# Block 0 of a fused attention and channel-mix kernel: v loaded at once and turned ahead of S, its copies shared by ScalarE and VectorE, and x of block 1 among the first up products

## The chip, the cores and the metric

The kernel runs on one core of a Trainium2 chip. The metric is the device time of one execution in microseconds, smaller is better; the profile's span (first to last instruction) is about 1.8 us less.

## The reference, cut to what matters

```python
# four batches, N = 6208 tokens, C = 256 channels
qn = q / (norm(q, axis=1) + 1e-6);  kn = k / (norm(k, axis=1) + 1e-6)
s = kn^T @ qn / tau                    # 256 x 256 for each batch
a = softmax(s, axis=-1)
x = v @ a                              # 6208 x 256
x_prev = x one token earlier (0 first)
xk = mu_k * x + (1 - mu_k) * x_prev;   xr likewise with mu_r
k = relu(xk @ w_k);  out = sigmoid(xr @ w_r) * (k * k @ w_v)
```

S needs all tokens of a batch, so the kernel first streams q and k of batch 0, and nothing of the channel mix can run before S, its softmax and the first x. After that blocks of 512 tokens pass through x, up (w_k), square and down (w_v), while S of the next batch is summed up beside them.

## The kernel before

These are the parts that the change touches. `take_half` copies half of the turned v out of PSUM, `product` makes x and its difference to the token before from the attention shares and v, `mix_first` makes xk and xr, `up_first` makes half a column block of the first up products, `x_half` makes half of x of a later block.

```python
def v_load(i):
    ...
    if i == 0:
        for a in range(2):
            nc.gpsimd.dma_start(v_bf[:, 2 * a:2 * a + 2], v[b, a * H:(a + 1) * H, :].rearrange(
                "(s p) c -> p s c", p=P))
        ...
def v_first():
    vT_ps = ps.tile([P, S, 2, P], BF16, name="vT_ps", tag="kT_ps", bufs=3)   # one PSUM bank
    def turn_half(a):
        for s in (2 * a, 2 * a + 1):
            for h in range(2):
                nc.tensor.transpose(vT_ps[:, s, h], v_bf[:, s, h * P:(h + 1) * P], ident)
    def take_half(a, copy):
        copy(vT0[:, :, a * H + 1:(a + 1) * H + 1].rearrange("c h (s p) -> c s h p", s=2),
             vT_ps[:, 2 * a:2 * a + 2])
...
# order of the loads on the GpSimd queue: v(0), v(1), w_k, q and k, w_r, v(2), w_v, v(3), ...
root(1); root(0)
nc.scalar.activation(gate, ones[:, 0:1], AF.Exp)     # loads the table for exp
turn_half, take_half = v_first()
invert_first(0)
evac_first()                  # VectorE scales S
turn_half(0)
turn()                        # TensorE turns S
turn_half(1)
keep_warm(2)
go = v_transpose_pe(1, nc.scalar.copy)
invert_first(1)
take_half(0, nc.vector.tensor_copy)
difference(0)
exp()
go()
weigh_first(0); weigh_first(1)
take_half(1, nc.vector.tensor_copy)
difference(1)
for a in range(2):
    for ih in range(2):
        product(a, ih)
    for dh in range(2):
        mix_first("xk", a, dh)
...
# main loop, round i == -1:
if i == -1 and j < 3:
    for fh, a in (((0, 0), (1, 0), (0, 1)), ((1, 1),), ())[j]:
        up_first(fh, a)
    if j == 2:
        up(0, 2)
...
if j in (0, 2) and full:
    x_half(n, int(j > 0))     # n = i + 2, here block 1
```

## Time and profile before

| what | value | from |
|---|---|---|
| time | 505.04 us, median of 4 runs, 504.71 to 505.17 | runs |
| span of the profiled run | 503.1 us | profile |
| TensorE busy | 482.3 us, 96% | page, part 1 |
| TensorE idle from 36 to 45 us | 1.93 us | busy time by stage |
| x of block 2 starts | 49.12 us | timeline |

The page's part 1 has each engine's busy time, part 4 the shares of the chain that ended last. Their lines, the table by stage and the chain are in the prediction below. The reading in short: the view of waits lists none of TensorE's matmuls from 49.3 to 480 us, so the change can gain only by starting that stream earlier, and at most the idle time ahead of it.

### The profile page before, as it was taken

The numbers are of one execution on the slowest core, as the hardware profiler recorded it, in microseconds if no ns is written. First come the engines' busy times: TensorE is split into PE (matmuls) and PEld (weight loads), VectorE is DVE, ScalarE is ACT, GpSimd is POOL, SyncE is SP. The second block draws the span as 40 slices with busy tenths as digits, with TensorE's granted clock in tenths as the row PEclk, the third lists the DMA queues.
The fourth block names the chain that finished last, engine by engine and source line by source line (L and its number), as shares of the span: only waits on it lengthen the run. The fifth ranks groups of instructions, "written<-read, shape, count | busy, mean of one in ns | idle before, by whom it ended". The sixth has DMA issues, their size and how long they took to land.

```text
span 503.1 us, 9303 instructions
## 1 busy us (share of the span) xinstructions
PE 482.3 (96%) x3437; PEld 331.2 (66%) x3437; DVE 429.7 (85%) x787; ACT 428.2 (85%) x871; POOL 96.9 (19%) x143
## 2 busy tenths in 40 slices
PE   2789999999999999999999999999999999999996
PEld 1355677677666766666776666676666666666675
DVE  2788899999988998999889899899888787878784
ACT  4788999899999989888999898988888888788884
POOL 0044322222233132122123323100031010000000
PEclk9999999999999999999999999999999999999999
DMA  8999999999799999997799999982295658344123
GB/s 328 418 314 197 196 185 176 209 210 195 149 187 179 202 166 177 146 203 116 142 191 146 197 171 183 168 150 65 66 207 103 152 86 156 77 105 86 56 71 106
DMA packets 131558, 83.46 MB, mean 166 GB/s; under 512 B 50548, under 2 KB 125624, under 8 KB 130488
## 3 DMA queue, kind: packets, MB, share of 16 engines
q0 software_dynamic: 55840, 33.01, 49.8%
q1 hardware_dynamic: 75352, 49.59, 39.9%
q8 instruction: 27, 0.44, 0.4%
q10 hardware_dynamic: 320, 0.26, 0.2%
q14 instruction: 19, 0.16, 0.1%
HBM read 78.71 MB, written 25.43 MB: 207 GB/s over the span
## 4 chain that ended last, share of the span: by engine, by line
PE 92%; DMA 4%; ACT 2%; DVE 1%; issue 0%; SPq 0%; ACTq 0%; DVEq 0%
PE vr_ps L603 33%; PE kT_ps L571 33%; PE vr_ps L599 8%; PE xT_ps L465 8%; PE s_ps L293 6%; DMA f<-in_k_dram 4%; ACT k L160 1%; PE s_ps L199 1%; ACT qk L155 1%; PE st_ps L353 0%; PE y_ps L643 0%; PE kT_ps L511 0%; PE bank L217 0%; PE vT_ps L425 0%; DVE xk L498 0%
## 5 line engine op out<-in xcount | busy, mean ns | idle before, releaser
L576 ACT ACTIVATE kr<-kT_ps 128x512 bf16<-128x512 f32 (+1 forms) x390 | 234.9, 604 | 33.4 <-PE kT_ps L571 29.7
L603 PE MATMUL vr_ps<-w_v_sb,kk 128*128 128x256 bf16 x1536 | 230.3, 273 | 0.0
L571 PE MATMUL kT_ps<-xk,w_k_sb 128*128 128x512 bf16 (+1 forms) x780 | 229.8, 377 | 0.0
L603 PEld LDWEIGHTS <-kk 128*128 128x128 bf16 x1536 | 150.3, 98 | 57.3
L584 DVE TENSOR_TENSOR kk<-kr 128x2048 bf16<-128x2048 bf16 (+1 forms) x148 | 125.7, 850 | 0.2 <-ACT kr L576 0.2
L613 DVE SCALAR_TENSOR_TENSOR res<-res,vr_ps 128x256 f32<-128x256 f32 x192 | 80.0, 416 | 50.1 <-ACT res L612 50.1
L571 PEld LDWEIGHTS <-w_k_sb 128*128 128x128 bf16 x780 | 75.5, 98 | 27.5 <-issue 0.6
L612 ACT ACTIVATE res<-vr_ps 128x256 f32<-128x256 f32 x192 | 76.7, 399 | 1.3 <-PE vr_ps L603 1.3
L599 PE MATMUL vr_ps<-w_r_sb,xr 128*128 128x256 bf16 x384 | 73.3, 273 | 0.0
L467 ACT CAST xT<-xT_ps 128x512 bf16<-128x512 f32 x94 | 55.9, 595 | 20.0 <-PE xT_ps L465 19.7
L556 DVE SCALAR_TENSOR_TENSOR xr<-delta,mu_t,xT 128x512 bf16<-128x512 bf16 x94 | 70.0, 746 | 0.0
L556 DVE SCALAR_TENSOR_TENSOR xk<-delta,mu_t,xT 128x512 bf16<-128x512 bf16 x94 | 70.0, 745 | 0.0
L599 PEld LDWEIGHTS <-xr 128*128 128x128 bf16 x384 | 37.6, 98 | 44.5 <-issue 0.2
L133 POOL DMA_DIRECT2D qk<-in_q_dram x39 | 26.0, 668 | 169.3 <-ACT kr L576 147.7
L465 PE MATMUL xT_ps<-vT,a_sb 128*128 128x512 bf16 x188 | 55.9, 379 | 0.0
L293 PE MATMUL s_ps<-qk 128*128 128x256 bf16 (+1 forms) x294 | 55.8, 273 | 0.0
L254 ACT ACTIVATE sq<-qk 128x1024 bf16<-128x1024 bf16 x48 | 51.0, 1063 | 0.0
L408 POOL DMA_DIRECT2D v_bf<-in_v_dram x47 | 35.6, 759 | 67.3 <-DMA vT<-v_bf 48.7
L199 PE MATMUL s_ps<-qk 128*128 128x384 bf16 (+2 forms) x98 | 20.2, 357 | 14.8 <-ACT qk L155 14.8
L546 DVE TENSOR_TENSOR delta<-xT 128x1024 bf16<-128x1024 bf16 x47 | 32.2, 686 | 1.1 <-ACT xT L467 1.1
L293 PEld LDWEIGHTS <-qk 128*128 128x128 bf16 (+1 forms) x294 | 28.5, 98 | 5.6 <-issue 0.8
L133 POOL DMA_DIRECT2D qk<-in_k_dram x39 | 25.9, 665 | 3.4 <-DMA w_k_sb<-in_moe_w_k_dram 2.0
(113 smaller groups left out, 252.7 us busy)
## 6 DMA issues: line engine op xcount, KB each, us to landing
out_dram<-res SPq DMA_DIRECT2D x47, 512.0 KB, 4.7
v_bf<-in_v_dram POOLq DMA_DIRECT2D x47, 256.0 KB, 7.3
qk<-in_q_dram POOLq DMA_DIRECT2D x36, 256.0 KB, 6.1
qk<-in_k_dram POOLq DMA_DIRECT2D x36, 256.0 KB, 7.3
f<-in_q_dram SPq DMA_DIRECT2D x4, 1024.0 KB, 13.3
f<-in_k_dram SPq DMA_DIRECT2D x4, 1024.0 KB, 11.0
f<-in_q_dram SPq DMA_DIRECT2D x3, 512.0 KB, 7.6
f<-in_k_dram SPq DMA_DIRECT2D x3, 512.0 KB, 6.2
```

What stands on the lines that cost most here:

```text
L133: nc.gpsimd.dma_start(rows_at(qk, b, g, i)[:rows, :n], qk_src(t, b, g))
L293: nc.tensor.matmul(s_ps[:, ih, :], rows_at(qk, b, g, 0)[:rows, s, ih * P:(ih + 1) * P], rows_at(qk, b, g, 1)[:rows, s, :], start=t0 and ih ...
L465: nc.tensor.matmul(xT_ps, a_sb[:, b, ih, dh * P:(dh + 1) * P], vT[:, :, ih, :], start=ih == 0, stop=ih == 1)
L467: nc.scalar.copy(xT[:, dh, 1:], xT_ps)
L556: nc.vector.scalar_tensor_tensor(o[:, dh], st[i, "d"][:, dh], mu[:, dh:dh + 1], st[i, "x"][:, dh, :M], op0=OP.mult, op1=OP.add)
L571: nc.tensor.matmul(kT_ps[:, :m], w_k_sb[:, dh, fh * P:(fh + 1) * P], xk[:, dh, :m], start=dh == 0, stop=dh == 1)
L576: nc.scalar.activation(kr, kT_ps[:, :m], AF.Relu, scale=0.5 ** 0.5)
L584: nc.vector.tensor_tensor(st[i, "kk"][:, fh // 4 * 4 + lo:fh + 1, :m], kr, kr, op=OP.mult)
L599: nc.tensor.matmul(vr_ps[:, D:], xr[:, dh, s * P:(s + 1) * P], w_r_sb[:, dh, :], start=dh == 0, stop=dh == 1)
L603: nc.tensor.matmul(vr_ps[:, :D], kk[:, fh, s * P:(s + 1) * P], w_v_sb[:, fh, :], start=fh == 0, stop=fh == 7)
L612: nc.scalar.activation(res[:, s], vr_ps[:, D:], AF.Tanh, scale=0.5)
L613: nc.vector.scalar_tensor_tensor(res[:, s], res[:, s], 1.0, vr_ps[:, :D], op0=OP.add, op1=OP.mult)
```

## The change

Its intent is to take the turning and the second copy of v off the path from S to the first products, and to fill TensorE's hole among the first up products with x of block 1. The diff is complete but for its context lines:

```diff
 def v_load(i):
-        if i == 0:
-            for a in range(2):
-                nc.gpsimd.dma_start(v_bf[:, 2 * a:2 * a + 2], v[b, a * H:(a + 1) * H, :].rearrange(
-                    "(s p) c -> p s c", p=P))
-            st[i, "v"] = v_bf
-            return
         nc.gpsimd.dma_start(v_bf, v[b, t * M:(t + 1) * M, :].rearrange(...))
...
     turn_half(0)
+    turn_half(1)
+    take_half(0, nc.scalar.copy)
     turn()
-    turn_half(1)
     keep_warm(2)
...
-    take_half(0, nc.vector.tensor_copy)
+    take_half(1, nc.vector.tensor_copy)
     difference(0)
...
-    take_half(1, nc.vector.tensor_copy)
     difference(1)
...
-                for fh, a in (((0, 0), (1, 0), (0, 1)), ((1, 1),), ())[j]:
+                for fh, a in (((0, 0), (1, 0)), ((1, 1),), ())[j]:
                     up_first(fh, a)
+                if j == 0:
+                    x_half(1, 0)
+                    up_first(0, 1)
...
-                if j in (0, 2) and full:
+                if j in (0, 2) and full and (i, j) != (-1, 0):
                     x_half(n, int(j > 0))
```

Below, parts (a) to (d) are those of the prediction: (a) one load, (b) both halves turned ahead of S, (c) ScalarE takes the first half, (d) x of block 1 among the up products.

## The prediction

> **What bounds the kernel now.** I read the page first, parts 1 and 4, for the engine that sets the end.
>
> ```profile
> PE 482.3 (96%) x3437; PEld 331.2 (66%) x3437; DVE 429.7 (85%) x787; ACT 428.2 (85%) x871; POOL 96.9 (19%) x143
> PE 92%; DMA 4%; ACT 2%; DVE 1%; issue 0%; SPq 0%; ACTq 0%; DVEq 0%
> ```
>
> TensorE is 92% of the chain that ended last. The view of waits, asked for TensorE alone from 49.3 to 480 us, lists no wait of a matmul at all, so from there on the kernel is one unbroken stream of matmuls. A change ahead of that stream can only move its start; whatever the start moves should reach the end unchanged. So I then asked for the busy time by stage around the change (columns: stretch, its length, busy us and instruction count of each engine, clock, DMA share, GB/s).
>
> ```profile
> 36.00:39.00 3.00, 2.22 (x23) 1.41 (x21) 2.44 (x8) 2.25 (x6) 3.00 (x5) 1.00 1.03 166
> 39.00:42.00 3.00, 2.26 (x22) 1.69 (x20) 2.37 (x9) 1.95 (x5) 0.82 (x2) 1.00 1.11 191
> 42.00:45.00 3.00, 2.59 (x16) 1.25 (x14) 2.92 (x8) 2.60 (x9) 1.56 (x3) 1.00 1.20 205
> 45.00:48.00 3.00, 3.00 (x24) 1.88 (x23) 1.94 (x3) 2.90 (x7) 1.02 (x2) 1.00 1.44 195
> ```
>
> Between 36 and 45 us TensorE is not full: 3.00 less 2.22, 2.26 and 2.59 leave 0.78 + 0.74 + 0.41 = 1.93 us idle. That is a ceiling on the gain (0.4% of the time). The clock is full throughout. Last I read the chain in order of time there (start, us, engine, tile, line).
>
> ```profile
> 37.38 0.83 PE st_ps L353 x4
> 38.20 0.24 PE vT_ps L444 x4
> 38.44 0.03 issue
> 38.47 0.44 DVE vT L447
> 38.90 0.02 issue
> 38.93 0.43 DVE delta L479
> ...
> 39.92 0.35 DVE a_sb L374
> 40.28 0.34 DVE vT L447
> 40.62 0.04 issue
> 40.66 0.50 PE x_ps L487 x3
> ...
> 42.84 0.39 ACT kr L513
> 43.23 0.04 issue
> 43.27 0.40 PE kT_ps L511 x2
> ```
>
> The turning of v (L444, after S is turned at L353) and both copies of it by VectorE (L447, at 38.47 and 40.19) are on the chain, and so is the wait of the first up product's second half (L511, 43.27) for ScalarE's relu at 42.84. These are the three things that the change touches.
>
> **What the Trainium skill says.** (1) "PSUM — Partial Sum Buffer", section PSUM bank collisions raise a hardware error, has the rule to guard PSUM with semaphores by bank, not by address. The trace agrees that such waits exist: the first half of v was turned by about 36.6, but its copy started at 38.47, just after the second half was turned at 38.44, in the same bank; and L511 at 43.27 waits for the relu of the other half of its own bank. (2) "ScalarE: Activation LUTs", section What ACT_TABLE_LOAD costs, gives 186 + 0.833 N ns for an instruction with immediate scale and bias: 613 ns for the new 128x512 copy (estimate). The trace agrees: 1.01 us for 128x1024 (the rule gives 1.04) and 0.59 for a 128x512 cast. (3) "DMA: Bandwidth & Descriptors", section Issuing engines are not separate DMA queues: all transfers share the 16 DMA engines. Here the DMA share is above 1.0 in every stage shown, so one issue instead of two saves issue time but hardly transfer time.
>
> **The change, part by part.** I write new times in the frame of the old trace and subtract at the end.
>
> (a) v of block 0 in one load. The old issues took 0.86 and 0.73 us from 31.88 and landed after 4.3 and 3.8 us, that is at 36.2 and 36.5. A whole load of the same pattern issues in about 0.75 (as the later ones do). The packets are the same and in the same order, so I take the landing as 36.0 to 36.5. Every later load is issued up to 0.8 us earlier; none of them is waited for now, so this gains nothing by itself.
>
> (b) Both halves turned ahead of S. Four turns issue in some 0.24 us (the chain's row of L444), eight in 0.45. From 36.5 that ends at about 36.95, with results near 37.15. S can be turned only at 37.38, when VectorE has scaled it. So this fits in idle TensorE time, with 0.4 us to spare, and takes 0.24 us out from behind L353.
>
> (c) The first half taken by ScalarE. It is free from the gate's exponential to exp:
>
> ```profile
> 37.33 0.21 ACT L741 ACTIVATE gate<-ones 128x1 bf16<-128x1 bf16 x1
> 38.27 0.47 ACT L361 ACTIVATE e_sb<-st_ps,rn 128x256 f32<-128x256 f32 x1 [0.73 <-PE st_ps L353]
> 43.71 0.38 ACT L513 ACTIVATE kr<-kT_ps 128x256 bf16<-128x256 f32 x1 [0.21 <-PE kT_ps L511]
> 44.14 0.59 ACT L467 CAST xT<-xT_ps 128x512 bf16<-128x512 f32 x1
> 48.07 1.01 ACT L433 COPY vT<-vT_ps 128x1024 bf16<-128x1024 bf16 x1
> ```
>
> From 37.54 a copy of 0.60 ends at 38.14; exp needs S turned, at 38.24. So it is hidden, by 0.1 us. VectorE copies the second half when its reciprocal ends (38.18) and ScalarE is out of the bank (38.14): start 38.20, not 38.47, a gain of 0.27. The difference starts at 38.66, the first reciprocal at 39.00, the first share at 39.19 (its exp and sum are ready at 38.83), the second share at 39.65, ending at 40.00. VectorE no longer has to copy v at 40.19. The products of the second shares (L487, 40.66) waited for that copy; now they wait for the share alone, 40.00 + 0.05 = 40.05. **Gain 0.61 us** (0.27 from the earlier start, 0.34 from the copy gone). The second difference ends near 40.36, before 40.49 when it is needed. The casts of x (L491), the four mixes of xk and the first up products follow at once, so all shift by 0.61; ScalarE's copy of v of block 1, which ends at 40.35, is out of the way of the first cast at 40.58.
>
> (d) x of block 1 between the up products. In the old frame the first four up products end their issue at 42.86. The next needs the relu at 43.23 and the fourth mix, at about 43.35: a hole of 0.4 us. The two products of x take 0.43 (L465 at 43.51 to 43.94) and fit in it. So the third pair goes at 43.29 to 43.51, the fourth to 43.75, the next up product to 44.18. The second x product waited at 44.78 for the cast that ended at 44.73 (same buffer). ScalarE now does that cast right after two relus, 43.55 to 44.14, so TensorE can go at 44.18: 0.60 earlier. But **ScalarE takes over as the limit**. From 42.84 it has the same sum of work in another order, and only its own hole of 0.21 us (before 43.71), with perhaps 0.1 of a later one, can close. It is then gapless to its copy of v of block 2, which moves from 48.07 to 47.76 and ends at 48.77. In the old trace x of block 2 started at 49.12, just after that copy ended at 49.08: no slack. Now it starts at 48.81 and TensorE waits there for about 0.29. So of 0.60 only **0.31 us** remain.
>
> The sum is 0.61 + 0.31 = 0.92 us. From 49 us on both engines shift alike and no transfer comes too late: the closest are w_k (34.00 + 7.0 = 41.0, needed at 41.5 after the shift), v of block 2 (36.48 + 9.1 = 45.6, needed at 46.3) and w_v (37.0 + 11.2 = 48.2, needed at 49.3). So 505.05 - 0.92 = 504.13; I say 504.2, as more small waits can appear than vanish.
>
> **The rivals.**
> 1. v lands late. S is now turned behind all of v, so TensorE would hold S until v is there. For: v used to land only 0.9 us ahead of S, while the DMA engines are over-subscribed, and the first half could start alone. Against: the same packets are queued 0.8 us earlier as to the second half. A landing at 37.5 instead of 36.5 would delay S by some 0.6 and eat part (c): about 504.7.
> 2. ScalarE does not bind. If the buffers of up products leave more slack than I see, part (d) keeps its 0.60: about 503.85. For: in the old trace TensorE never waits after 45 us. Against: the 0.04 us between the end of the copy and x of block 2.
> 3. ScalarE's copy delays exp. It has 0.1 us of slack; if the copy takes 0.8 rather than 0.6, exp and all behind it slip by 0.1 and the second copy, kept out of the bank, too: about 504.35.
> 4. The gain is given back later, to the transfers: the DMA share is 1.44 at 45 to 48 us and some rows of q and k land 2 to 3 us ahead of use. A stream that starts 0.9 earlier has that much less slack. Against: no wait of TensorE from 49.3 to 480. It would leave 504.6 to 505.
>
> **Range and chances.** Rivals 1, 3 and 4 bound the small gains, rival 2 the large. The three old runs lie within 0.14 us, so noise is not the issue. I take 503.7 to 504.8 as the range. A change of 2% is 10 us, while all idle time of TensorE in these stages is 1.93 us: faster by 2% is out of the question, and slower by 2% would take a wait on each of many blocks, which the change does not touch. Faster 0.01, within 2% 0.98, slower 0.01.
>
> **What would show it.** In the new profile: v landing before 36.9 and L444 as one run of eight ahead of L353 at about 37.38; one ScalarE copy of 0.6 us between the gate and exp, with exp still near 38.27; one VectorE copy at 38.2; the second group of L487 near 40.05; x of block 1 (L465) directly behind four L511 and no wait for ScalarE at the fifth; ScalarE gapless from 42.2 to 60; the ScalarE copy of v of block 2 near 47.15 (48.07 - 0.92); and a matmul stream without waits after 49. Wrong would be: S turned later than 37.5, exp later than 38.4, a wait for DMA on TensorE, or a start of x of block 2 later than 48.4, with the time above 504.8.

## The result, and the profile after

The changed kernel took 503.74 us (median of 4 runs, 503.54 to 503.94) against 505.04. The ratio is 0.9975, 95% interval 0.9958 to 0.9993. Ratios here are the mean time of one kernel's runs over that of the other's of the same rounds, so not quite the ratio of the medians quoted. The gain of 1.30 us by the medians is larger than the 0.84 predicted, and the time lies inside the range, near its lower end.

Single executions of both kernels scatter more than the first runs showed. In all four sets the kernel before had medians of 504.85 to 505.07, but single runs up to 508.53; the changed kernel's three sets had medians of 503.74, 503.97 and 504.26, that is 1.30, 1.05 and 0.59 us under the kernel before of the same set. So the gain is about 1 us, and the prediction's 0.84 is not separable from it. The first and third sets of experiments ran on one chip, the second (load_only, rows4, both_dve, act_extra) on another and without the changed kernel beside it, so its kernels are compared through the kernel before.

All lines of the new kernel from the load of v on are numbered six lower (L444 is now L438, L511 is L505, and so on). First the page of the changed kernel, parts 1 and 4:

```profile
PE 478.7 (95%) x3378; PEld 331.0 (66%) x3437; DVE 428.6 (85%) x786; ACT 429.0 (85%) x872; POOL 96.7 (19%) x142
PE 91%; DMA 4%; ACT 2%; DVE 1%; issue 1%; SPq 0%; ACTq 0%; DVEq 0%
```

Some matmul records are missing from this trace (3378 of 3437, while all weight loads are there), so TensorE's lower busy time says nothing. Then its busy time by stage, columns as before:

```profile
36.00:39.00 3.00, 2.37 (x25) 1.58 (x24) 2.44 (x11) 2.97 (x9) 2.57 (x5) 1.00 1.00 156
39.00:42.00 3.00, 2.28 (x18) 1.52 (x18) 2.26 (x9) 2.17 (x7) 0.55 (x2) 1.00 1.09 202
42.00:45.00 3.00, 2.94 (x17) 1.65 (x17) 2.44 (x7) 2.88 (x10) 1.50 (x3) 1.00 1.20 203
45.00:48.00 3.00, 2.95 (x24) 2.01 (x24) 2.80 (x4) 3.00 (x7) 1.58 (x3) 1.00 1.43 196
```

TensorE's hole from 42 to 45 us is nearly closed (2.94 where it was 2.59): that is part (d). Ahead of 42 us it has nearly the holes of before, in other places. The chain in order of time shows them (start, us, engine, tile, line):

```profile
37.57 0.21 ACT gate L735
37.77 0.51 ACT vT L441
38.28 0.02 issue
38.31 0.44 DVE vT L441
38.74 0.02 issue
38.77 0.43 DVE delta L473
...
39.72 0.97 PE x_ps L481 x7
...
41.12 0.89 DVE xk L492 x2
42.01 0.04 issue
42.05 0.49 PE kT_ps L505 x3
42.54 0.43 PE xT_ps L459 x2
```

The second copy at 40.28 and the turning behind S are gone, but ScalarE's copy now stands on the chain ahead of VectorE's. The timeline of the changed kernel shows why, and what S waited for:

```profile
36.77 0.88 DVE L332 TENSOR_SCALAR s_sb<-s_ps,rn 128x256 f32<-128x256 f32 x2
37.03 0.62 PE L438 MATMUL vT_ps<-ident,v_bf 128*128 128x128 bf16 x8 [0.58 <-DMA v_bf<-in_v_dram]
37.49 0.65 PE L353 MATMUL st_ps<-ident_f,s_sb 128*128 128x128 f32 x4
38.31 0.43 DVE L441 COPY vT<-vT_ps 128x512 bf16<-128x512 bf16 x1 [0.35 <-ACT vT L441]
```

v came at 37.0, not by 36.5. TensorE turned v first, as the program orders it, and S at 37.49, that is 0.72 after VectorE began to scale S; in the kernel before it was 37.38 - 36.84 = 0.54. So S was 0.18 late. And VectorE waited 0.35 us for ScalarE to leave the bank.

The gain can be read in three intervals, which the starts in the timelines give: the **front**, from the scaling of S (L332) to the first mix of xk; the **middle**, from there to x of block 2; and the **tail**, from there to the end of the span. "S late" is the start of S's turning (L353) less that of its scaling, less the 0.54 of the kernel before.

| kernel | S late | front | middle | tail | span |
|---|---|---|---|---|---|
| before | 0 | 41.60 - 36.84 = 4.76 | 49.12 - 41.60 = 7.52 | 453.98 | 503.1 |
| changed | 0.18 | 41.12 - 36.77 = 4.35 | 48.06 - 41.12 = 6.94 | 454.14 | 502.2 |

Front 0.41, middle 0.58, tail -0.16, and S's scaling 0.07 earlier: together 0.90, the difference of the spans. The same table for the experiments follows them.

### The profile page after: what moved, and what is told of

Same layout as the page of the kernel before. It is cut to its first block, busy times and chain, and to the rows that moved or that the text cites. A ratio compares the mean times of both kernels' runs of the same rounds, so it can differ in the third digit from the quotient of the medians.

```text
span 502.2 us, 9243 instructions
## 1 busy us (share of the span) xinstructions
PE 478.7 (95%) x3378; PEld 331.0 (66%) x3437; DVE 428.6 (85%) x786; ACT 429.0 (85%) x872; POOL 96.7 (19%) x142
## 4 chain that ended last, share of the span: by engine, by line
PE 91%; DMA 4%; ACT 2%; issue 1%; DVE 1%; SPq 0%; ACTq 0%; DVEq 0%
PE vr_ps L597 33%; PE kT_ps L565 31%; PE vr_ps L593 10%; PE xT_ps L459 8%; PE s_ps L293 6%; DMA f<-in_k_dram 4%; ACT k L160 1%; PE s_ps L199 1%; ACT qk L155 1%; PE y_ps L637 0%; PE st_ps L353 0%; ACT L735 0%; PE vT_ps L419 0%; PE x_ps L481 0%; PE kT_ps L505 0%
## 5 line engine op out<-in xcount | busy, mean ns | idle before, releaser
L565 PE MATMUL kT_ps<-xk,w_k_sb 128*128 128x512 bf16 (+1 forms) x722 | 217.3, 377 | 0.0
L593 PEld LDWEIGHTS <-xr 128*128 128x128 bf16 x384 | 37.6, 98 | 44.6 <-issue 0.2
L402 POOL DMA_DIRECT2D v_bf<-in_v_dram x48 | 36.8, 767 | 97.9 <-DMA vT<-v_bf 49.3
```

The lines of the kernel that those rows point to most:

```text
L565: nc.tensor.matmul(kT_ps[:, :m], w_k_sb[:, dh, fh * P:(fh + 1) * P], xk[:, dh, :m], start=dh == 0, stop=dh == 1)
L593: nc.tensor.matmul(vr_ps[:, D:], xr[:, dh, s * P:(s + 1) * P], w_r_sb[:, dh, :], start=dh == 0, stop=dh == 1)
```

## The experiments

Twelve experiments ran, in three sets. The kernel before ran beside each, with medians of 505.02 (first set), 505.07 (second) and 504.85 us (third). All gave right results.

### after_again and after_third: the changed kernel again

No edit.

> The changed kernel once more, as the yardstick for the three runs beside it on the same chip. Expected: 1.2 to 1.4 us under the kernel before, as in the result on record (503.74 against 505.04). Its profile should tell whether the late start of the softmax of batch 0 in the first profile of the changed kernel (the norms end at 35.97 us, 35.74 in the kernel before; the last loads of q and k landed 0.5 us later) belongs to the change or to that one execution: if to the change, it is again near 36.0; if to the execution, near 35.7.

> The changed kernel a third time, beside the two candidates, and one more sample of the landing of one whole load. So far six executions with one load of 512 rows of v had it at 36.3, 37.0, 37.0, 37.4, 37.7 and 37.7 us, and the three with two loads had all that they waited for by 36.5. Theory L (one load is systematically later): v at 37.0 or later again. Rival (the execution's luck, through the backlog of the q and k loads): by 36.5 as likely as not. Time: 503.7 to 504.0 us.

after_again: 503.97 us, ratio 0.9981 (0.9967 to 0.9995). after_third: 504.26 us, ratio 0.9990 (0.9977 to 1.0002), so by itself its set does not settle a difference. The late start of the softmax in the first execution (scaling of S at 36.77) does not belong to the change: it began at 36.60 and 36.59 in these. v came at 37.0 in the one and at 36.6 in the other, and S was late by 0.37 and by 0. The fronts are 4.59 and 4.36 and the middles 6.93 and 6.94. after_third started its stream earliest of the three, x of block 2 at 47.89, and yet its span is 502.3: its tail is 0.43 longer than before, of which 0.24 is one wait that the timeline shows (start, length, engine, line, tile, and the idle time before with its releaser):

```profile
78.39 0.59 PE L459 MATMUL xT_ps<-vT,a_sb 128*128 128x512 bf16 x2 [0.24 <-DMA vT<-v_bf]
```

The transposing load for this block was issued at 61.02 and landed 17.3 us later; in the kernel before its like was issued at 62.14 and landed after 12.9. In the other twelve traces it landed after 12.7 to 17.2 us. So a transfer that had 4 us of slack (62.14 + 12.9 = 75.0, needed at 79.10) is now sometimes the next limit.

### d_only: part (d) alone

The kernel before with the last three pieces of the diff.

```diff
-                for fh, a in (((0, 0), (1, 0), (0, 1)), ((1, 1),), ())[j]:
+                for fh, a in (((0, 0), (1, 0)), ((1, 1),), ())[j]:
                     up_first(fh, a)
+                if j == 0:
+                    x_half(1, 0)
+                    up_first(0, 1)
...
-                if j in (0, 2) and full:
+                if j in (0, 2) and full and (i, j) != (-1, 0):
```

> The kernel before with only the reordering of x of block 1 among the first up products. Theory A (ScalarE had slack, and the part is worth what the wait view and the hole say): 0.55 to 0.6 us faster than the kernel before, the second product of x of block 1 and x of block 2 both 0.6 earlier. Theory B (as predicted: ScalarE takes over): x of block 1 is 0.6 earlier, x of block 2 only 0.3, and the time falls by 0.3.

504.67 us, ratio 0.9988 (0.9976 to 1.0). The front is the old one (4.76), and the middle fell by only 0.14 to 7.38. That looks like theory B, but the timeline names another cause:

```profile
42.58 0.61 PE L511 MATMUL kT_ps<-xk,w_k_sb 128*128 128x256 bf16 x4 [0.65 <-DMA w_k_sb<-in_moe_w_k_dram]
```

w_k landed at 42.54 in this execution, not at 41.0 as in the profile of before, and the first up products waited for it. From these four to x of block 2 it is 48.77 - 42.58 = 6.19 us, without a wait, so ScalarE did not bind here. Neither number of the two theories came true.

### no_d: parts (a) to (c) without (d)

The changed kernel with the three pieces of d_only taken back.

> The changed kernel without the reordering: only the load at once, both halves turned ahead of S, and the copies shared. Theory A: 0.6 to 0.75 us faster than the kernel before, and 0.55 to 0.6 slower than the changed one. Theory B: 0.6 faster than before, and 0.3 slower than the changed one (which would leave 0.4 of the measured 1.3 unexplained).

505.13 us, ratio 0.9998 (0.9983 to 1.0013): no gain at all. In its trace v landed at 37.7, later than in any profile before:

```profile
37.73 0.62 PE L438 MATMUL vT_ps<-ident,v_bf 128*128 128x128 bf16 x8 [1.22 <-DMA v_bf<-in_v_dram]
```

S was turned at 38.19, 0.83 late, and the front became 5.01, longer by 0.25 than before. The middle is 7.52, exactly that of before. So without (d) the middle is 7.52 and with it 6.94, whatever the front does: **part (d) is worth 0.58 us**. (The medians of no_d and after_again, of the same set, are 1.16 us apart. Their traces differ by 1.1, of which 0.42 is the front, longer in no_d as v came later.) Of the two theories A is right about this term and wrong about the front.

### halves: the changed kernel with v in two loads

```diff
+        if i == 0:
+            for a in range(2):
+                nc.gpsimd.dma_start(v_bf[:, 2 * a:2 * a + 2], ...)
+            st[i, "v"] = v_bf
+            return
```

> The changed kernel, but v of block 0 in two loads as before. Theory L (one load lands later than two: 37.0 us in the changed kernel's profile against 36.2 and 36.5, and S was turned 0.19 us after its scaling was done): v lands by 36.6, S is turned as soon as it is scaled, and the time is 0.15 to 0.25 us under the changed kernel. Rival (the late landing was that execution's, as its loads of q and k were late too): v lands within 0.2 us of the landing in the repeat of the changed kernel, and the times agree within 0.1 us.

504.63 us, ratio 0.9987 (0.9975 to 0.9999). The theory of the landing seemed right: the halves were there at 36.1 and 36.5, S was late by 0, and the front is 4.33. But the time was no better than the changed kernel's (504.63 against 503.97 in the same set). In the trace w_k took v's place:

```profile
41.83 0.61 PE L511 MATMUL kT_ps<-xk,w_k_sb 128*128 128x256 bf16 x4 [0.52 <-DMA w_k_sb<-in_moe_w_k_dram]
```

Two issues for v put that of w_k at 34.05, against 33.7 in the changed kernel, and it landed at 41.8. The middle is 7.24. Later it also waited for the transposing load, issued at 61.09 and landing 17.2 us later.

### load_only: part (a) alone

The kernel before without the branch for block 0 in the load of v.

> The kernel before with v of block 0 in one load and nothing else. Theory L (one load lands later than two; three whole loads so far landed at 37.0, 37.0 and 37.7 us, three pairs of halves by 36.5): v lands at 37 to 37.7, the first four turns wait for it, S is turned up to 0.5 us after it is scaled, and the time is 0 to 0.4 us above the kernel before. Rival (the load's form doesn't matter): v by 36.5, S turned at once, same time.

504.85 us, ratio 0.9988 (0.9964 to 1.0012): not told apart from the kernel before. In the trace v was at 37.7, S 0.59 late, and the front 5.13, longer by 0.37, with the span at 503.4. So the trace shows the loss that was expected, and the times don't resolve it.

### rows4: v with four neighbouring rows in a partition

```diff
-            "(p s) c -> p s c" if i in (1, 2) else "(s p) c -> p s c", p=P))
+            "(p s) c -> p s c" if i in (0, 1, 2) else "(s p) c -> p s c", p=P))
...
-            copy(vT0[:, :, a * H + 1:(a + 1) * H + 1].rearrange("c h (s p) -> c s h p", s=2),
-                 vT_ps[:, 2 * a:2 * a + 2])
+            copy(vT0[:, :, a * H + 1:(a + 1) * H + 1].rearrange("c h (p s) -> c h p s", s=S),
+                 vT_ps[:, :, :, a * P // 2:(a + 1) * P // 2].rearrange("c s h p -> c h p s"))
```

> The changed kernel, but v of block 0 loaded with four neighbouring rows of 256 in each partition, as v of blocks 1 and 2 is, and put in order by the two copies (strided on VectorE and ScalarE). Theory P (the queue of the casting loads moves so many packets in a time, not so many bytes): a quarter of the packets for v, so v lands by 36.5, S is turned as soon as it is scaled, w_k lands 0.3 to 0.5 us earlier than the 41.7 of the changed kernel, the VectorE copy takes up to 0.2 longer, and the time is 0.2 to 0.6 under the changed kernel. Rival (bytes or order set the landing): v at 37.0 again, w_k at 41.7, and the time is the changed kernel's or 0.1 to 0.2 above it for the strided copies.

504.40 us, ratio 0.9982 (0.9958 to 1.0006), with the best trace of all (span 502.0) and two of six executions over 505.5. v was at 36.2, w_k at 41.0 and S not late. From 34.3 to 37.0 us the casting queue moved 0.44 MB in 246 packets, against 0.47 MB in 591 packets in the changed kernel. So it does not move a fixed number of packets in a time, and theory P fails in its reason. The landings that it foretold came true all the same, but v took 4.4 us from issue to landing just as in act_extra, which has the form of the changed kernel, and w_k was issued earlier (32.99 against 33.74) and landed after 8.0 us against 7.9. And VectorE pays for the strided copy:

```profile
36.21 0.62 PE L438 MATMUL vT_ps<-ident,v_bf 128*128 128x128 bf16 x8
...
37.95 0.69 DVE L441 COPY vT<-vT_ps 128x512 bf16<-128x512 bf16 x1
```

The copy takes 0.69 where it took 0.43, and the front is 4.59, 0.25 longer than act_extra's with v as early. The times don't show it to beat the changed kernel.

### both_dve: both halves copied by VectorE

```diff
     turn_half(1)
-    take_half(0, nc.scalar.copy)
     turn()
...
+    take_half(0, nc.vector.tensor_copy)
     take_half(1, nc.vector.tensor_copy)
     difference(0)
```

> The changed kernel with both halves copied by VectorE, one after the other, behind its reciprocal and ahead of the differences; ScalarE copies none. In the changed kernel VectorE waited 0.35 to 0.54 us for ScalarE's copy (same bank), so two copies of 0.43 from 37.96 would end at 38.85, against 38.74. Theory A (the gain of part b and c is from taking the copy of the second half off the time after the shares; who copies matters little): 0.1 us slower than the changed kernel. Rival (as predicted, ScalarE's help brings 0.27 of it): 0.3 to 0.45 slower.

504.03 us, ratio 0.9971 (0.9949 to 0.9993). By the medians it is 1.04 us under the kernel before, within the changed kernel's 0.59 to 1.30; the ratio is lower since two runs of the kernel before in this set took 506.60 and 508.53. v was at 37.4, S 0.56 late:

```profile
38.09 0.89 DVE L441 COPY vT<-vT_ps 128x512 bf16<-128x512 bf16 x2
```

From the turning of v (37.44) to the end of the copies it is 38.98 - 37.44 = 1.54 us; in the changed kernel 38.74 - 37.03 = 1.71. So when v is late, VectorE alone is 0.17 faster, since a copy by ScalarE of 0.59 stands ahead of its own rather than beside it. The front is 4.58, and at a lateness of 0.56 that is 0.2 better than after_again's 4.59 at 0.37 would let expect. That fits theory A; with v early both_dve has no trace, so whether ScalarE's help pays then is not shown.

### act_extra: half a microsecond more for ScalarE

```diff
                 up(i + 1, j)
+                if (i, j) == (-1, 3):
+                    nc.scalar.copy(spare, fill)
```

(The line that makes the tile `spare` is cut.)

> The changed kernel with one more copy of 128x512 on ScalarE (some 0.5 us, into a spare tile) behind the fourth relu of block 0. Theory A (ScalarE has slack there, since in the kernel before it waited for TensorE inside a merged row of relus): x of block 2 is at most 0.1 later and the time the same. Theory B (the reordering has used ScalarE's slack up; its copy of v of block 2 ends at 48.02 us and x of block 2 starts at 48.06): x of block 2 is 0.4 to 0.5 later and so is the end. Either way it says how much of the reordering's 0.58 us a busier ScalarE would have taken.

504.20 us, ratio 0.9976 (0.9954 to 0.9998). Here v was at 36.3 and the front 4.34, but the middle is 7.43, longer by 0.49 than with (d) alone. From the second product of x of block 1 to x of block 2, first in this kernel and then in the changed one:

```profile
43.46 0.59 PE L460 MATMUL xT_ps<-vT,a_sb 128*128 128x512 bf16 x2
48.30 0.59 PE L460 MATMUL xT_ps<-vT,a_sb 128*128 128x512 bf16 x2
```

```profile
43.72 0.59 PE L459 MATMUL xT_ps<-vT,a_sb 128*128 128x512 bf16 x2
...
48.06 0.59 PE L459 MATMUL xT_ps<-vT,a_sb 128*128 128x512 bf16 x2
```

That is 4.84 against 4.34: the copy's 0.5 us (ScalarE's next instruction starts 0.51 after it) comes out in full. Theory B is right that ScalarE has no slack left after the change, though reaching this point cost nothing.

### halves_w_k and whole_w_k: w_k in two loads

```diff
-    nc.gpsimd.dma_start(w_k_sb, moe_w_k.rearrange("(ko ki) f -> ki ko f", ki=P))
+    for f in (slice(0, DF // 2), slice(DF // 2, DF)):
+        nc.gpsimd.dma_start(w_k_sb[:, :, f], moe_w_k.rearrange("(ko ki) f -> ki ko f", ki=P)[:, :, f])
     next_load()
-    nc.gpsimd.dma_start(w_r_sb, moe_w_r.rearrange("(ko ki) d -> ki ko d", ki=P))
     v_load(2)
+    nc.gpsimd.dma_start(w_r_sb, moe_w_r.rearrange("(ko ki) d -> ki ko d", ki=P))
```

The first is halves with this edit, the second the changed kernel with it.

> The changed kernel with v of block 0 in two loads, w_k in two loads of 512 columns each (the first up products need only the first), and w_r behind v of block 2. Theory W (with v in two loads the wait for v is replaced by one for w_k, which is issued 0.5 us later: the first up product waited for w_k at 41.83 and 42.58 us in the two kernels with two loads and the reordering): now v lands by 36.5, w_k's first half by 40.8, no up product waits for a load, the first starts 4.8 us after the scaling of S does, and the time is 0.3 to 0.6 under the changed kernel. Rival (some other load takes the place, most likely v of block 1 at 38.7 or of block 2 at 46.3, as the queue moves the same bytes): the time is that of the changed kernel within 0.2 us, with a wait of TensorE for one of these.

> The changed kernel with w_k in two loads of 512 columns and w_r behind v of block 2, v of block 0 in one load. Theory W: with the whole load it is v that binds and w_k lands just in time (41.7), so the split gains at most 0.1 us; 503.6 to 504.0. Rival (w_k costs the changed kernel more than its profile shows, in other executions than the profiled one): 0.2 to 0.4 us under the changed kernel.

halves_w_k: 504.39 us, ratio 0.9988 (0.9974 to 1.0001). whole_w_k: 504.12 us, ratio 0.9984 (0.9972 to 0.9997). Neither is shown to beat the changed kernel of the same set (504.26, 0.9990). In halves_w_k the second half of v came at 37.3, though it was a load by itself, so two loads do not make all of v early; whether one load is later on the average stays open. The first half of w_k landed at 41.8 in spite of the split, and v of block 2 became a wait:

```profile
46.84 0.62 PE L425 MATMUL vT_ps<-ident,v_bf 128*128 128x128 bf16 x8 [0.28 <-DMA v_bf<-in_v_dram]
```

In whole_w_k v was at 37.6, S 0.77 late, and the front 4.95. The rival of the first expectation, that another load takes the place, came true.

### before_again: the kernel before, one look

No edit.

> The kernel before once more, one look, for a further sample of the landing with two loads (36.2 and 36.5 us in the profile of before) and of w_k (41.0). Theory L: both halves by 36.6. Rival (luck): one of them at 37 or later. In either case the first four turns start near 36.2 and S is turned 0.54 us after its scaling starts, as only the first half is ahead of it.

505.12 us, one run. The first half of v was at 36.4, and S was not late. TensorE turned the second half at 37.95 without a wait, so it was there by then, but no record says when. w_k landed at 42.56, and the first up products waited 0.55 us for it; the kernel before lost 0.27 of that (middle 7.79), as its mixes of xk were only just done.

### All traces side by side

v is the time at which its first turns start, in kernels with two loads that of the first half.

| kernel | v | S late | front | middle | tail |
|---|---|---|---|---|---|
| before | 36.20 | 0 | 4.76 | 7.52 | 453.98 |
| before_again | 36.41 | 0 | 4.76 | 7.79 (w_k late) | 454.00 |
| d_only | 36.15 | 0 | 4.76 | 7.38 (w_k late) | 454.03 |
| load_only | 37.68 | 0.59 | 5.13 | 7.53 | 453.96 |
| no_d | 37.73 | 0.83 | 5.01 | 7.52 | 453.95 |
| changed | 37.03 | 0.18 | 4.35 | 6.94 | 454.14 |
| after_again | 37.05 | 0.37 | 4.59 | 6.93 | 454.08 |
| after_third | 36.61 | 0 | 4.36 | 6.94 | 454.41 |
| halves | 36.08 | 0 | 4.33 | 7.24 (w_k late) | 454.28 |
| rows4 | 36.21 | 0 | 4.59 | 6.94 | 454.03 |
| both_dve | 37.44 | 0.56 | 4.58 | 6.94 | 454.09 |
| act_extra | 36.29 | 0.01 | 4.34 | 7.43 | 454.00 |
| whole_w_k | 37.63 | 0.77 | 4.95 | 6.94 | 454.04 |
| halves_w_k | 36.10 | 0.46 | 4.65 | 7.39 (v of block 2 late) | 454.40 |

## Why the prediction was right or wrong

The time, the direction and the size were right. Of its working some steps held and some did not: parts (b) and (c) were priced about 0.2 us too high with v in time, and more with v late, and part (d) 0.27 too low. That the sum came out near is to that extent luck.

**What bounds the kernel, and that a start moves the end: right.** The tail is 454.0 us, within 0.2, in eleven of the fourteen traces. In after_third, halves and halves_w_k it is 0.3 to 0.4 longer, with a wait for a late transfer named by the timeline or the chain in each (a transposing load in the first two, w_v in the third).

**(a), v by 36.0 to 36.5: wrong, and the most important error.** The step "the packets are the same and in the same order, so I take the landing as 36.0 to 36.5" failed. In eight executions with one load of this form v came at 36.3, 36.6, 37.0, 37.0, 37.4, 37.6, 37.7 and 37.7 us. It is a spread of 1.4 us, where the plan had 0.4 to spare. Where v came at 37 or later, S was turned late, by 0.18 to 0.83 us: rival 1, which was priced at 0.6 for a landing at 37.5, is what happened in most of them. What sets the landing is open. It is not simply one load instead of two: a second half came at 37.3 in halves_w_k. The traces hold one hint. In the three of the eight executions in which the scaling of S began at 36.53 to 36.60, v was issued at 31.87 to 31.95 and came at 36.3, 36.6 and 37.0; in the five in which it began at 36.77 to 36.82, v was issued at 32.11 to 32.16 and came at 37.0 to 37.7. The scaling needs the last of q and k, so v seems to be late when they are; no experiment tested it. The kernel before is less exposed, since only its first half stands ahead of S, and that came at 36.1 to 36.4 in every execution with two loads.

**(b) and (c), 0.61 us: too large.** With v in time the front fell from 4.76 to 4.33 to 4.36, that is by 0.40 to 0.43 us, in halves, act_extra and after_third. The term of 0.34 for the vanished second copy nearly held; the term of 0.27 for an earlier first copy did not. From the scaling of S to VectorE's first copy it was 38.47 - 36.84 = 1.63 us before and 38.05 - 36.53 = 1.52 in act_extra, so 0.11 of the 0.27 came, and from that copy to the first mix of xk it was 3.13 and 2.82, a gain of 0.31.

The failed step is "ScalarE is out of the bank (38.14)", that is ahead of VectorE. VectorE waited for ScalarE by 0.35 us in the changed kernel, 0.54 in after_again, and still 0.36 in act_extra, where v was in time. The Trainium skill's "PSUM — Partial Sum Buffer" (section PSUM bank collisions raise a hardware error) has it that two engines must be kept apart in a bank, on the same partitions, even when both only read. Both copies read all 128 partitions of one bank, and the traces agree that they are kept apart: VectorE's starts 0.03 us after ScalarE's ends, at 38.31 and 38.28 in the changed kernel. I counted that wait, but with ScalarE's copy ending 0.04 us ahead of VectorE's turn; in act_extra it ended 0.33 behind it.

Both times were read from one atypical profile. In act_extra ScalarE's copy started 37.45 - 36.53 = 0.92 us after the scaling of S began; I had 37.54 - 36.84 = 0.70, as a tiny add of VectorE ahead of that scaling (L325) took 0.47 us in that profile, where it took 0.17 in all thirteen other traces. And its second add took 0.34, where it took 0.16 in act_extra, so that VectorE was free 1.16 us after the scaling began and not 1.34. The copy itself was as estimated (0.57 to 0.59, estimate 0.60). In the traces of the changed kernel and no_d with v late, the front gained 0.17 to 0.41 or lost up to 0.25.

**Rival 3, exp delayed by ScalarE's copy: no.** With S turned late, exp started 0.68 us after S's turning did in the changed kernel (38.17 - 37.49), and 0.65 after it in load_only and both_dve, where ScalarE copies no half of v. With S in time it was 0.86 in act_extra and 0.87 in before_again.

**(d), 0.60 in the first place: right.** The hole was filled as told, and the middle fell by 0.58 us in every trace with the reordering that lost nothing to a late load or to the extra copy. **The 0.29 taken off for ScalarE: wrong**, so rival 2 was right. The failed step is "only its own hole of 0.21 us (before 43.71), with perhaps 0.1 of a later one, can close". I read four relus of ScalarE as one gapless piece since the timeline had merged them in one row. Asked for shorter stretches, the view of the kernel before shows that the last of the four starts later than its turn:

```profile
46.86 1.31 ACT L576 ACTIVATE kr<-kT_ps 128x512 bf16<-128x512 f32 x2
```

```profile
47.57 0.60 ACT L576 ACTIVATE kr<-kT_ps 128x512 bf16<-128x512 f32 x1
```

Two starts 0.71 apart, where the others follow in about 0.5: ScalarE waited some 0.2 us for its up product, which TensorE had finished at 47.53. Also its hole before 43.71 is 0.31 by the starts (the two relus at 42.84 took 0.66 together and 0.38 each, so they follow in 0.28, and the third's turn was at 42.84 + 0.56 = 43.40), not the 0.21 that the wait view lists. ScalarE had thus half a microsecond to give, and its copy of v of block 2 moved from 48.07 to 47.01, as much as TensorE's work. That it is now full is shown by act_extra.

**No other transfer too late: wrong for w_k.** It was taken from one landing at 41.0. In the traces it came at 41.0 to 42.6, and in d_only, halves and before_again it cost 0.27 to 0.44 us of the middle. v of block 2 cost about 0.45 in halves_w_k. That a transposing load would be the one to give some of the gain back (rival 4 in kind) was not seen: 0.24 us in after_third.

So in the three traces of the changed kernel the sum 0.61 + 0.31 = 0.92 came about as roughly 0.2 to 0.4 in front, 0.58 in the middle, and 0.1 to 0.4 given back in the tail, while the scaling of S, from which the front is counted, began anywhere from 36.44 to 36.84 in the fourteen traces. Part (d) is the firm share of the gain; parts (a) to (c) pay only when v is early.

## What to carry to other kernels

Before you put work that needs a load ahead of the critical step on an engine that takes its work in the program's order, as TensorE did here, look at the landing in several executions, not in one: a spread of a microsecond turns a spare hole into a wait. Two engines that emptied the same PSUM bank took turns here, at 0.35 to 0.54 us of waiting; giving one engine all of it cost nothing that the times show, and one bank each was not tried. And before you call an engine gapless, ask for the start of every instruction; a merged row hides the waits inside it.

## What the Trainium skill lacked or had wrong

- "DMA: Bandwidth & Descriptors", section Anatomy of one DMA — SWDGE (gpsimd) path: its fit of 2.0 us + bytes / 436e3 gives an estimate of 2.6 us for the 256 KB of v and 3.2 us for the 512 KB of w_k (bytes as they land; in HBM they are twice as many). Here, with a DMA share of 0.84 to 1.36 around them (changed kernel, 31.5 to 38.5 us), v in one load took 4.4 to 5.5 us from issue to landing and w_k 7.0 to 8.3. The page has no word on the spread between executions, and it was the spread that decided.
- The same page, section DMA Transpose (X-bar), gives no time; elsewhere the page has only a bandwidth, and nothing on the time from issue to landing beside other transfers. The transposing load of 128x1024 elements landed 12.9 us after its issue in the kernel before and 17.3 us after it in after_third.
- "PSUM — Partial Sum Buffer", section PSUM bank collisions raise a hardware error, has ScalarE and VectorE kept apart in one bank, and the traces agree that they were; no run shows what happens otherwise. It does not say what follows for a shared emptying: VectorE waited 0.35 to 0.54 us for ScalarE's 0.59 us copy, and VectorE alone was 0.17 us faster when v was late.
